# Splitting 49 output matmuls, moving the keys-values burst, and spreading the last stores in an attention-plus-MoE kernel

## Chip, cores, metric

One core of one Trainium2 chip. The metric is device time in microseconds (us). Before the change: 296.5 us (median of four runs, 296.09 to 296.61). All times are of fast runs unless said otherwise.

## The reference

```python
# attention: batch 8, heads 8, 576 positions, head size 64
r = np.maximum(x, 0.0); phi(x) = concat([r * cos_w, r * sin_w])      # for q and k
kv  = einsum('bhsf,bhsd->bhfd', phi(k), v);  z = sum(phi(k), axis=2)
x   = einsum('bhsf,bhfd->bhsd', phi(q), kv) / (einsum('bhsf,bhf->bhs', phi(q), z) + 1e-6)
# then, on 4608 tokens of 512:
h = x @ w_in                                # 512 -> 2048
g = h * (1 / (1 + exp(-beta * h)))
out = g @ w_out                             # 2048 -> 512, float32
```

## The kernel before

The 4608 tokens go in nine chunks of 512, numbered 0 to 8. For each chunk TensorE computes h in 16 *slots* (four matmuls of 512 columns each), ScalarE makes g of it, and TensorE forms the output. In chunks 0 and 1 the output is a plain product (`o_mm`); from chunk 2 on it is two fast products of seven sub-products each (`o_fast`, Strassen's scheme, 112 matmuls of 256 columns). In between stands the attention of the next batch: the keys-values burst `kv_all` (72 small matmuls), the numerators `num_all` (144), and the quotients `x_part` on VectorE. `raw_q` is the load of a later batch's q, and the `qt` transposes turn q by DMA. In `o_fast`, `m1` to `m7` are the seven products (x for the first pair of token tiles, y for the second), and `a3` to `a7` are VectorE's additions that combine their results, which TensorE leaves in banks of PSUM, its result memory. Of the code, `...` marks what is left out.

```python
def store(c, tt, o_sb, m0=0, m1=DM):
    for hf in range(2):
        bb, n = divmod((c * TCH + tt * P) // HP + hf, NQ)
        if c < 7 or (c == NTC - 1 and tt == 1):
            eng = nc.gpsimd
        else:
            eng = (nc.sync, nc.scalar)[hf] if (c, tt) == (NTC - 1, 3) else nc.sync
        eng.dma_start(out=out_v[bb, n][:, m0:m1], in_=o_sb[hf * HP : (hf + 1) * HP, m0:m1])

def o_mm(c, tt, jts):
    o_ps = ps[:, (2, 3, 0, 1)[tt] if c == 0 else 2 + tt % 2]
    for jt in jts:
        nc.tensor.matmul(o_ps, lhsT=gs[c, jt // 4][:, jt % 4, tt * P : (tt + 1) * P],
                         rhs=wout[:, jt, :], start=(jt == 0), stop=(jt == JT - 1))
    ...                                                   # copy and store when the last part is done

def att_q(b):
    q_relu(b, 0); q_relu(b, 1)
    q_turn_dma(b)                                         # transposes qb into qt, by DMA
    if b + 1 < B:
        load_raw(b + 1, "q")                              # 1152 KB

for slot in range(32):                                    # chunk 1
    if slot < 16:
        h_group(1, slot)
    else:
        o_part(1, (slot - 16) // 4, slot % 4)             # four o_mm steps
    one_unit(slot)

for c in range(2, NTC):
    b = c + 1
    for slot in range(16):
        h_group(c, slot)
        if slot == 0 and b < B:
            k_all(b); v_half(b, 1)
        if slot == 3 and b + 1 < B:
            att_q(b + 1)
        ...                                               # g_sums in slots 3, 7, 11, 13, 15
        if slot == 12 and b < B:
            kv_all(b)
    x, y = o_fast(c, 0, 6), o_fast(c, 1, 7)
    if b < B:
        for t, bank in enumerate((6, 0, 4)):
            num_all(b, t, bank)
        ...
        x_part(b, 0, 6)
    for n in (1, 5, 6, 2, 7, 3):
        x[f"m{n}"]()
        if n == 5 and b < B:
            x_part(b, 1, 0)
        if n == 6:
            x["a5"](); x["a6"]()
            if b < B:
                x_part(b, 2, 4)
    ...
```

## Time and profile before

| What | Before | How to read it |
|---|---|---|
| Time | 296.5 us | profiled run: span 294.5 us from first to last instruction |
| First numerator to next chunk's h, chunks 2 to 6 | 15.40, 15.94, 18.60, 14.27, 14.14 us | equal work, so every difference is waiting or a lower clock |
| TensorE gaps ahead of the fast products put down to "issue" | 6.7 us | "issue" means that the profile shows nothing that it waited for |
| TensorE clock | 0.5 from 165.18 to 168.59 us | the one slow slice of the run's middle |
| VectorE's last instruction to the common end | 6.3 us | 288.19 to 294.49 us |

The lines themselves stand in the prediction.

### The profile page before, as it was taken

The numbers are of one execution on the slowest core, as the hardware profiler recorded it, in microseconds if no ns is written. First come the engines' busy times: TensorE is split into PE (matmuls) and PEld (weight loads), VectorE is DVE, ScalarE is ACT, GpSimd is POOL, SyncE is SP. The second block draws the span as 40 slices with busy tenths as digits, with TensorE's granted clock in tenths as the row PEclk, the third lists the DMA queues.
The fourth block names the chain that finished last, engine by engine and source line by source line (L and its number), as shares of the span: only waits on it lengthen the run. The fifth ranks groups of instructions, "written<-read, shape, count | busy, mean of one in ns | idle before, by whom it ended". The sixth has DMA issues, their size and how long they took to land.

```text
span 294.5 us, 8004 instructions
## 1 busy us (share of the span) xinstructions
PE 276.2 (94%) x3369; PEld 174.8 (59%) x3376; DVE 197.4 (67%) x502; ACT 137.0 (47%) x228; POOL 75.7 (26%) x91
## 2 busy tenths in 40 slices
PE   8799999999999899989998699999999999999990
PEld 7454455455445585558645584578458845864780
DVE  5889975859996759675867469586858325424530
ACT  5678856861166314731384016621662177137510
POOL 1444000551760444035401424063400220000001
PEclk9999999999999999999999799999999999999997
DMA  7999999999999754984499246915301520050032
GB/s 250 376 392 373 394 344 358 293 269 322 245 252 302 218 121 97 321 235 96 88 361 237 56 98 177 297 31 126 73 2 29 125 73 0 20 124 1 2 72 71
DMA packets 50516, 53.94 MB, mean 183 GB/s; under 512 B 31200, under 2 KB 31472, under 8 KB 50480
## 3 DMA queue, kind: packets, MB, share of 16 engines
q1 hardware_dynamic: 47504, 45.69, 53.0%
q0 software_dynamic: 2784, 7.61, 9.9%
q8 instruction: 26, 0.43, 0.6%
q10 hardware_dynamic: 192, 0.14, 0.2%
q14 instruction: 10, 0.08, 0.1%
HBM read 36.71 MB, written 9.44 MB: 157 GB/s over the span
## 4 chain that ended last, share of the span: by engine, by line
PE 80%; DVE 9%; issue 5%; DMA 3%; SPq 1%; ACT 0%; POOL 0%; POOLq 0%; ACTq 0%; DVEq 0%
PE ps L374 41%; PE ps L440 28%; PE ps L420 5%; DMA raw_v<-in_v_dram 3%; PE ps L268 3%; PE ps L289 2%; DVE xs L311 2%; DVE vb L218 2%; DVE T L399 1%; SPq L79 1%; DVE rden L304 1%; DVE T L398 1%; DVE qb L193 0%; PE ps L348 0%; DVE win L115 0%
## 5 line engine op out<-in xcount | busy, mean ns | idle before, releaser
L374 PE MATMUL ps<-xt,win 128*128 128x512 bf16 (+1 forms) x580 | 127.3, 378 | 0.6 <-DVE vb L218 0.5
L382 ACT ACTIVATE g_t<-ps,beta 128x512 bf16<-128x512 f32 x144 | 98.6, 688 | 50.4 <-PE ps L374 48.3
L374 PEld LDWEIGHTS <-win 128*128 128x128 bf16 x580 | 56.0, 98 | 65.5 <-DMA xt<-xs 1.0
L415 POOL DMA_DIRECT2D out_dram<-o_sb x58 | 36.1, 629 | 127.6 <-issue 101.0
L440 PEld LDWEIGHTS <-S 128*128 128x128 bf16 x448 | 44.1, 99 | 11.4 <-issue 5.6
L221 POOL TENSOR_TENSOR qs<-qt,tanr 128x1152 bf16<-128x1152 bf16 x12 | 28.8, 2419 | 69.9 <-DVE den L300 55.6
L391 DVE TENSOR_TENSOR S<-g_t 128x512 bf16<-128x512 bf16 (+1 forms) x35 | 13.0, 371 | 37.5 <-ACT g_t L382 37.5
L440 PEld LDWEIGHTS <-g_t 128*128 128x128 bf16 x336 | 32.9, 99 | 6.8 <-issue 2.1
L440 PE MATMUL ps<-T,S 128*128 128x256 bf16 x224 | 28.1, 277 | 4.9 <-issue 4.9
L440 PE MATMUL ps<-wout,g_t 128*128 128x256 bf16 x224 | 30.1, 278 | 1.8 <-issue 1.8
L420 PE MATMUL ps<-wout,g_t 128*128 128x512 bf16 x121 | 28.3, 379 | 0.6 <-issue 0.3
L440 PE MATMUL ps<-wout,S 128*128 128x256 bf16 x224 | 27.0, 274 | 0.1
L470 ACT COPY o_sb<-ps 128x256 f32<-128x256 f32 x14 | 5.2, 372 | 46.3 <-PE ps L440 46.3
L311 DVE TENSOR_TENSOR xs<-ps,rden 128x768 bf16<-128x768 f32 (+4 forms) x26 | 22.8, 884 | 0.8
L218 DVE TENSOR_SCALAR vb<-raw_v,cos 128x256 bf16<-128x256 f32 x63 | 22.3, 402 | 0.0
L420 PEld LDWEIGHTS <-g_t 128*128 128x128 bf16 x128 | 12.1, 98 | 13.7
L460 ACT COPY p<-ps 128x256 f32<-128x256 f32 x14 | 5.2, 373 | 25.5 <-PE ps L440 25.5
L218 DVE TENSOR_SCALAR vb<-raw_v,sin 128x256 bf16<-128x256 f32 x54 | 14.7, 347 | 0.0
L440 PE MATMUL ps<-T,g_t 128*128 128x256 bf16 x112 | 14.5, 273 | 0.0
L394 DVE TENSOR_TENSOR S<-g_t,S 128x512 bf16<-128x512 bf16 (+1 forms) x35 | 13.0, 372 | 1.2
L497 DVE TENSOR_TENSOR o_sb<-ps,p 128x256 f32<-128x256 f32 x14 | 5.9, 425 | 11.3 <-PE ps L440 11.3
L289 PEld LDWEIGHTS <-qt 64*64 64x64 bf16 x576 | 10.4, 106 | 4.9 <-issue 3.7
(76 smaller groups left out, 238.5 us busy)
## 6 DMA issues: line engine op xcount, KB each, us to landing
raw_v<-in_v_dram SPq DMA_DIRECT2D x7, 1152.0 KB, 9.3
raw_k<-in_k_dram SPq DMA_DIRECT2D x7, 1152.0 KB, 7.6
raw_q<-in_q_dram SPq DMA_DIRECT2D x7, 1152.0 KB, 6.2
out_dram<-o_sb POOLq DMA_DIRECT2D x58, 128.0 KB, 2.7
w_stage<-in_moe_w_in_dram SPq DMA_DIRECT2D x3, 1024.0 KB, 14.0
w_stage<-in_moe_w_out_dram SPq DMA_DIRECT2D x2, 1024.0 KB, 7.6
w_stage<-in_moe_w_out_dram SPq DMA_DIRECT2D x4, 512.0 KB, 11.9
out_dram<-o_sb SPq DMA_DIRECT2D x12, 128.0 KB, 2.3
```

Source lines behind the costliest of these rows:

```text
L218: nc.vector.tensor_scalar(o, a, scalar1=t[:, n : n + 1], scalar2=None, op0=ALU.mult)
L221: return eng.tensor_tensor(dst.rearrange("q n (g p) -> q n g p", g=2), src.rearrange("q n (g p) -> q n g p", g=2), tanr[:, n0:n1].unsqueez ...
L268: nc.tensor.matmul(t[jj * HP : (jj + 1) * HP, g], lhsT=rk[hs, n, 2 * jp + jj, :], rhs=vb[hs, n, 2 * jp + jj].rearrange("q s e -> q (s e)") ...
L289: nc.tensor.matmul(ps[cols, bank + jj, slot * E : (slot + 1) * E], lhsT=(qts[b % 2], qs)[cs][rows, jp, n, cols], rhs=kv[rows, g, jp, cs, : ...
L311: nc.vector.tensor_tensor(o.rearrange("q j n s d -> q j (n s) d"), nv[:, :, a:z, :, 0:D].rearrange("q j n s d -> q j (n s) d"), rden[:, :, ...
L374: nc.tensor.matmul(ps[:, h_bank(c, jt), blocks.start * 64 : blocks.stop * 64], lhsT=win[jt // 4][:, mi, (jt % 4) * P : (jt % 4 + 1) * P], ...
L382: nc.scalar.activation(gs[c, jt // 4][:, jt % 4], ps[:, h_bank(c, jt)], AF.Silu, scale=beta[:, jt : jt + 1])
L391: nc.vector.tensor_tensor(s1, A21, A22, op=ALU.add)
L394: return nc.vector.tensor_tensor(s4, A12, s2, op=ALU.subtract)
L415: eng.dma_start(out=out_v[bb, n][:, m0:m1], in_=o_sb[hf * HP : (hf + 1) * HP, m0:m1])
L420: nc.tensor.matmul(o_ps, lhsT=gs[c, jt // 4][:, jt % 4, tt * P : (tt + 1) * P], rhs=wout[:, jt, :], start=(jt == 0), stop=(jt == JT - 1))
L440: nc.tensor.matmul(dst, lhsT=left(i), rhs=right[:, i], start=start and i == 0, stop=stop and i == JT // 2 - 1, skip_group_check=True)
```

## The change

Three edits. Forty-nine of chunk 1's output matmuls are cut into two column halves; `kv_all` goes from after h slot 12 to after h slot 10; the next-to-last tile of the last chunk is stored by SyncE and ScalarE in place of GpSimd. Neither of the first two removes work: the split adds 49 weight loads and 49 matmuls.

```diff
-            if c < 7 or (c == NTC - 1 and tt == 1):
-                eng = nc.gpsimd
-            else:
-                eng = (nc.sync, nc.scalar)[hf] if (c, tt) == (NTC - 1, 3) else nc.sync
+            eng = nc.gpsimd if c < 7 else (nc.sync, nc.scalar)[hf] if c == NTC - 1 and tt % 2 else nc.sync
-    def o_mm(c, tt, jts):
+    def o_mm(c, tt, jts, cols=1):
-            nc.tensor.matmul(o_ps, lhsT=..., rhs=wout[:, jt, :],
-                             start=(jt == 0), stop=(jt == JT - 1))
+            w = DM // cols if jt > 0 else DM
+            for m0 in range(0, DM, w):
+                nc.tensor.matmul(o_ps[:, m0 : m0 + w], lhsT=..., rhs=wout[:, jt, m0 : m0 + w],
+                                 start=(jt == 0), stop=(jt == JT - 1 and m0 == DM - w))
...                                                       # o_part hands cols on to o_mm
-            o_part(1, (slot - 16) // 4, slot % 4)
+            o_part(1, (slot - 16) // 4, slot % 4, 2 if slot > 18 else 1)
-            if slot == 12 and b < B:
+            if slot == 10 and b < B:
                 kv_all(b)
```

More of the change, by code (lines that the diff above doesn't have):

```diff
@@ L410, in store @@
             bb, n = divmod((c * TCH + tt * P) // HP + hf, NQ)
-            if c < 7 or (c == NTC - 1 and tt == 1):
-                eng = nc.gpsimd
-            else:
-                eng = (nc.sync, nc.scalar)[hf] if (c, tt) == (NTC - 1, 3) else nc.sync
+            eng = nc.gpsimd if c < 7 else (nc.sync, nc.scalar)[hf] if c == NTC - 1 and tt % 2 else nc.sync
             eng.dma_start(out=out_v[bb, n][:, m0:m1], in_=o_sb[hf * HP : (hf + 1) * HP, m0:m1])
-    def o_mm(c, tt, jts):
+    def o_mm(c, tt, jts, cols=1):
         o_ps = ps[:, (2, 3, 0, 1)[tt] if c == 0 else 2 + tt % 2]
         for jt in jts:
-            nc.tensor.matmul(o_ps, lhsT=gs[c, jt // 4][:, jt % 4, tt * P : (tt + 1) * P],
-                             rhs=wout[:, jt, :],
-                             start=(jt == 0), stop=(jt == JT - 1))
+            w = DM // cols if jt > 0 else DM
+            for m0 in range(0, DM, w):
+                nc.tensor.matmul(o_ps[:, m0 : m0 + w], lhsT=gs[c, jt // 4][:, jt % 4, tt * P : (tt + 1) * P],
+                                 rhs=wout[:, jt, m0 : m0 + w],
+                                 start=(jt == 0), stop=(jt == JT - 1 and m0 == DM - w))
         if jts[-1] < JT - 1:
@@ L427, in o_mm, with o_part @@
         store(c, tt, o_sb)
-    def o_part(c, tt, part):
-        o_mm(c, tt, range(4 * part, 4 * part + 4))
+    def o_part(c, tt, part, cols=1):
+        o_mm(c, tt, range(4 * part, 4 * part + 4), cols)
     def o_fast(c, pr, b_bank):
```

## The prediction

> **What bounds the kernel now.** I read the page's busy shares first, then who waited for whom, then the chain of waits piece by piece through chunks 2 to 4, then the windows by chunk, then the DMA queues and the end of the run.
>
> ```profile
> PE 276.2 (94%) x3369; PEld 174.8 (59%) x3376; DVE 197.4 (67%) x502; ACT 137.0 (47%) x228; POOL 75.7 (26%) x91
> PEclk9999999999999999999999799999999999999997
> q8 instruction: 26, 0.43, 0.6%
> ```
>
> TensorE is the bound: 94% busy, at full clock but for one slice in the middle. So the question is which TensorE gaps the change removes. Queue 8 matters later: 26 packets of 16 KB, 0.43 MB. From the waits:
>
> ```profile
> PE ps L440 <- issue: 6.7, 4, 3.0
> ```
>
> L440 holds the fast output products of chunks 2 to 8. TensorE stood still before them for 6.7 us in four pieces, and nothing visible released it: no semaphore, only "issue". The chain shows where three pieces lie (start, us, what):
>
> ```profile
> 97.40 1.36 PE ps L289 x137
> 98.76 3.06 PE ps L440 x26
> 101.82 1.35 issue
> 103.17 9.56 PE ps L440 x86
> ...
> 129.16 2.08 PE ps L440 x17
> 131.24 1.90 issue
> 133.14 10.53 PE ps L440 x95
> ...
> 160.10 1.09 PE ps L440 x9
> 161.19 2.99 issue
> 164.18 13.09 PE ps L440 x103
> ```
>
> The reader should look at the matmul counts before each gap: 26, 17, 9. A fourth gap of 0.45 us follows in chunk 5 after the first row of L440. Each matmul has a weight load, so these are about 52, 35, 18 and 1 instructions into L440: 17 fewer per chunk. The built program says why. One chunk has 785 TensorE instructions (h 128, keys-values 144, numerators 288, fast products 224, one semaphore), and 785 = 3 x 256 + 17. Numbering all TensorE instructions, the four gaps fall at places 194 to 195 modulo 256. So the gaps are the edges of 256-instruction blocks[...]. TensorE waits for its **own instructions**. The trace's records of queue 8 agree: packets start at 100.75, 130.66, 161.91 and 191.69, work resumes at 103.17, 133.14, 164.18 and 194.14, thus 2.3 to 2.5 us after the packet's start (about 1.0 us of it the packet itself).
>
> The windows give what this costs per chunk, from the first numerator to the next chunk's h (window, PE, PEld, DVE, ACT, POOL busy, PEclk, DMA share, GB/s):
>
> ```profile
> 97.33:112.73 15.40, 14.05 (x258) 12.29 (x258) 10.64 (x31) 2.18 (x5) 6.85 (x6) 1.00 0.55 145
> 127.73:143.67 15.94, 14.04 (x258) 12.37 (x258) 10.72 (x31) 2.18 (x5) 6.86 (x6) 1.00 0.52 143
> 158.66:177.26 18.60, 15.61 (x258) 13.17 (x258) 10.83 (x31) 2.18 (x5) 6.85 (x6) 0.91 0.44 117
> 192.25:206.52 14.27, 13.82 (x258) 12.46 (x258) 10.58 (x31) 2.17 (x5) 6.86 (x6) 1.00 0.37 81
> 221.51:235.65 14.14, 14.05 (x258) 12.39 (x258) 8.46 (x23) 2.18 (x5) 2.07 (x4) 1.00 0.37 81
> ```
>
> Same work each time. Chunk 6 has no instruction gap and takes 14.14 us. Its one gap, about 0.3 us before the seventh product, waits for VectorE's a6. Chunk 4 pays twice: 2.99 us of gap, then 3.41 us at half clock (the clock record is 0.5 from 165.18 to 168.59).
>
> [...]the trace behaves as if one block is fetched ahead.
> [...]in chunks 2 to 4 its packet starts only as the 1152 KB load of raw_q runs dry (100.7, 130.6, 161.7)[...].
> [...]Only the longest gap, 2.99 us, is followed by a half-clock stretch, of 3413 ns.
> [...]Here 64 L420 matmuls take 13.83 us (216 ns each) and 16 L440 matmuls of 256 columns 1.74 us (109 ns).
>
> **The change, part by part.**
> *Split.* 49 L420 matmuls of chunk 1 become 98 with 98 weight loads: 98 more TensorE instructions before chunk 2. Direct cost: 49 x (2 x 109 - 216) = 49 x 2 ns = 0.1 us; a weight load of 98 ns fits beside a 109 ns matmul. Its real effect is that each later block edge falls 98 instructions earlier in the work.
> *Keys-values burst.* It goes from after h slot 12 to after slot 10; its inputs are long ready (in chunk 3 VectorE ends the sine scaling at 117.1, slot 10 ends near 122). No work is added. Before the numerators 40 h instructions instead of 24 now stand, 20 matmuls x 216 ns = 4.32 us instead of 2.6 us, so an edge crossed near the burst leaves more time.
> I counted the new places in the built program. In chunks 2, 3, 4, 5, 6 the edge is numerator instruction 242, 225, 208, 191, 174 of 288; the edge before it is 14, 31, 48, 65, 82 instructions ahead of the numerators. The sequencer runs some 50 instructions ahead of TensorE (my estimate, from late fetches with quiet DMA), so the fetch starts about 64 instructions ahead in chunk 2, in the tail of the burst: 4.5 us before the numerators. The edge is reached 242/288 x 1.36 = 1.1 us into them. That leaves 5.7 us, where before chunk 2 had (98.76 + 3.06 - 97.4) = 4.4 us. Needed: 2.4 us plus the start of the packet, so it must start within about 3.3 us. What it meets is not raw_q, which comes about 2 to 4 us later, but the qt transposes (92.5 to 96.7 in chunk 2). A packet that waits for all of them starts near 97, would be usable at 99.4, and is needed at 98.5: up to 0.9 us lost in chunk 2, less in 3 and 4, nothing in 5 and 6; the first 0.4 us of each costs nothing, since the VectorE wait of chunk 6 absorbs it. I take 0.3 us in all.
> Gain against the 14.14 us chunk: 1.26 + 1.80 + 4.46 + 0.13 = 7.65 us. Chunk 4's 4.46 is the gap and the half clock together.
> *Stores.* The next-to-last store (chunk 8, tile 1) leaves GpSimd for SyncE and ScalarE. In the chain's end:
>
> ```profile
> 287.86 0.52 POOL out_dram L415
> 288.38 0.51 POOLq L814
> ```
>
> The trace shows GpSimd's closing drain from 288.28 to 293.71, while SyncE has seen all its own stores land by 291.66 and waits. The common end follows 0.75 us later, at 294.5. With GpSimd's last store in chunk 7, its drain should be over long before, and SyncE sets the end: 291.66 + 0.75 = 292.4. The new issues (0.47 to 0.55 us each, near 287.35) are done before the last halves are due at 288.2. Gain: 2.05 us.
> Sum: -7.65 - 2.05 + 0.3 + 0.1 = -9.3 us. 296.56 - 9.3 = **287.3 us**.
>
> **The rivals.**
> A: *the wait only moves.* The fetch, caught behind the transposes and then raw_q, arrives late inside the numerators. For it: in chunk 2 a fetch behind raw_v started its packet only at 92.66[...]. Against it: the earlier burst buys 1.7 us, and edges later in the sequence of chunks are ever safer. It would give back 1 to 2 us in each of chunks 2 to 4: 290 to 293 us, more if a half-clock stretch comes with it.
> B: *VectorE takes over.* Without gaps the a6 wait of chunk 6 may appear in every chunk. I have included it by taking 14.14 us; if VectorE falls back further, 0.3 us a chunk: 288.5 us.
> C: *no instruction fetch at all, only DMA or VectorE timing*, and the split is a plain cost. Then only the stores gain: about 294.6 us. The modulo-256 match of four gaps speaks strongly against it.
> D: *the end doesn't move*, because the stores land later on the two hardware queues: 289.3 us.
>
> **Range and chances.** All gaps gone, with a slightly better end: 286. One or two chunks keep a gap of 1 us, or the end fails: 290. So 285.9 to 290.2. Over 2% faster means below 290.6: 0.84. Within 2% needs rival A in force or C: 0.14. Slower needs new gaps longer than the old: 0.02.
>
> **What would show it.** Right: "issue" before L440 drops from 6.7 us to under 1; no half-clock slice before the end; chunks 2 to 6 alike at 14.0 to 14.5 us; queue 8 packets in each chunk starting before the numerators; the chain ending in SyncE or ScalarE, with 4 to 5 us between the last matmul and the end instead of 7. Wrong: gaps inside the numerators (L289) at places 194 modulo 256, raw_q again ahead of the fetch, or the last drain still about 5 us.

The trace of the kernel before shows this of blocks and fetches. Queue 8, of kind "instruction", moved 26 packets of 16384 bytes while 6745 matmuls and weight loads were recorded, one packet for 259. From the packet of chunk 2's gap to that of chunk 3's, 768 instructions on (785 less 17), there are three: 100.75, 104.80 and 121.45, then 130.66. Counting back 256 instructions from each gap gives the edge before it: in chunks 2 to 4 the packet starts 3.06, 2.66 and 3.04 us after TensorE reaches that edge. In chunk 6, where the packet at 219.63 is all that the DMA queues move from 214 to 222 us, it starts 1.95 us before TensorE is there, some 33 instructions ahead. The trace doesn't show when a fetch is asked for; the 50 instructions of the prediction are an estimate: these 33, and what TensorE gets through in the unknown time from the asking to the packet's start.

## The result, and the profile after

The changed kernel takes 285.36 us (median of four, 284.85 to 285.78), against 296.5 us before: ratio 0.9626, 95% interval 0.9607 to 0.9645. A ratio here is the mean time of one kernel's fast runs over that of the other's of the same rounds, so not quite the ratio of the medians. The prediction said 287.3 us with a range of 285.9 to 290.2. Its direction and mechanism held; the gain was larger than its range allowed.

The page of the changed kernel, busy shares and TensorE clock:

```profile
PE 275.7 (97%) x3425; PEld 178.9 (63%) x3425; DVE 197.8 (70%) x502; ACT 137.0 (48%) x228; POOL 74.7 (26%) x89
PEclk9999999999999999999999999999999999999999
```

TensorE does the same 276 us of work in a shorter span, and no slice is below 90% of the clock. From the table of waits, after:

```profile
PEld L439 <- issue: 1.3, 5, 0.3
PE ps L374 <- DMA xt<-xs: 0.8, 1, 0.8
```

L439 is the line that was L440. Its matmuls no longer wait for "issue" at all; what is left of it is five small waits of weight loads. The windows from the first numerator to the next h, chunks 2 to 6, columns as in the prediction:

```profile
97.20:111.33 14.13, 14.04 (x258) 12.39 (x258) 10.55 (x31) 2.18 (x5) 6.86 (x6) 1.00 0.54 145
126.32:140.45 14.13, 14.04 (x258) 12.38 (x258) 10.54 (x31) 2.18 (x5) 6.86 (x6) 1.00 0.48 131
155.44:169.57 14.13, 14.04 (x258) 12.37 (x258) 10.55 (x31) 2.18 (x5) 6.86 (x6) 1.00 0.50 126
184.56:198.69 14.13, 14.04 (x258) 12.37 (x258) 10.55 (x31) 2.18 (x5) 6.85 (x6) 1.00 0.42 82
213.69:227.81 14.12, 14.04 (x258) 12.37 (x258) 8.44 (x23) 2.18 (x5) 2.07 (x4) 1.00 0.45 81
```

All five are alike. The sum went from 78.35 to 70.64 us, a gain of 7.71 us.

The chain of waits in chunk 3, after (start, us, what):

```profile
126.43 0.70 ACT g_t L382
...
130.76 0.41 DVE p L481
131.17 0.34 DVE u L484
131.55 8.89 PE ps L439 x80
```

Where "issue" pieces stood, the chain now runs over ScalarE's last g, VectorE's sums, quotients, a5 and a6 into the seventh product: the short wait that only chunk 6 showed before. The end of the chain, after:

```profile
275.96 3.94 PE ps L439 x36
279.91 0.02 issue
279.93 0.42 DVE o_sb L496
```

VectorE's last instruction ends at 280.36 us and the span at 283.75: 3.39 us instead of 6.30, a gain of 2.91 us. The other parts of the span hardly move: the start of chunk 2's h goes from 82.18 to 82.05 us, the last two chunks take 52.55 instead of 52.54 us. So 7.71 + 2.91 + 0.1 = 10.7 us, which is the difference of the two spans (294.49 to 283.75).

### The profile page after: what moved, and what is told of

Same layout as the page of the kernel before. It is cut to its first block, busy times and chain, and to the rows that moved or that the text cites.

```text
span 283.7 us, 8110 instructions
## 1 busy us (share of the span) xinstructions
PE 275.7 (97%) x3425; PEld 178.9 (63%) x3425; DVE 197.8 (70%) x502; ACT 137.0 (48%) x228; POOL 74.7 (26%) x89
## 4 chain that ended last, share of the span: by engine, by line
PE 76%; DVE 12%; DMA 6%; issue 3%; ACT 1%; SPq 1%; DVEq 0%
PE ps L374 43%; PE ps L439 24%; PE ps L419 5%; DVE xs L311 3%; DMA raw_v<-in_v_dram 3%; PE ps L268 3%; DMA xt<-xs 2%; DVE rden L304 1%; ACT g_t L382 1%; DVE T L399 1%; SPq L79 1%; DVE p L481 1%; PE ps L289 1%; DVE T L398 1%; DVE den L300 1%
## 5 line engine op out<-in xcount | busy, mean ns | idle before, releaser
L412 POOL DMA_DIRECT2D out_dram<-o_sb x56 | 35.1, 632 | 69.8 <-issue 43.2
L439 PEld LDWEIGHTS <-S 128*128 128x128 bf16 x448 | 43.8, 98 | 7.0 <-issue 1.3
L439 PEld LDWEIGHTS <-g_t 128*128 128x128 bf16 x336 | 32.5, 98 | 4.3
L419 PE MATMUL ps<-wout,g_t 128*128 128x256 bf16 (+1 forms) x177 | 29.3, 320 | 0.0
L439 PE MATMUL ps<-wout,g_t 128*128 128x256 bf16 x224 | 29.1, 273 | 0.0
L439 PE MATMUL ps<-T,S 128*128 128x256 bf16 x224 | 27.3, 272 | 0.0
L439 PE MATMUL ps<-wout,S 128*128 128x256 bf16 x224 | 26.7, 272 | 0.4
L419 PEld LDWEIGHTS <-g_t 128*128 128x128 bf16 x177 | 16.9, 98 | 9.2
L439 PE MATMUL ps<-T,g_t 128*128 128x256 bf16 x112 | 14.5, 273 | 0.0
L289 PEld LDWEIGHTS <-qt 64*64 64x64 bf16 x576 | 10.4, 106 | 4.9 <-issue 3.7
```

The lines of the kernel that those rows point to most:

```text
L289: nc.tensor.matmul(ps[cols, bank + jj, slot * E : (slot + 1) * E], lhsT=(qts[b % 2], qs)[cs][rows, jp, n, cols], rhs=kv[rows, g, jp, cs, : ...
L419: nc.tensor.matmul(o_ps[:, m0 : m0 + w], lhsT=gs[c, jt // 4][:, jt % 4, tt * P : (tt + 1) * P], rhs=wout[:, jt, m0 : m0 + w], start=(jt == ...
L439: nc.tensor.matmul(dst, lhsT=left(i), rhs=right[:, i], start=start and i == 0, stop=stop and i == JT // 2 - 1, skip_group_check=True)
```

## The experiments

The theory under test: TensorE's instructions are fetched in blocks of 256 (one packet for 259 recorded), about one block ahead; a fetch waits in the DMA queues behind the data that is there (2.66 to 3.06 us in chunks 2 to 4 of before); the numerators (288 instructions in 1.36 us) use up a block faster than a late fetch brings the next (2.3 to 2.5 us from a packet's start to use); and the split matters only by moving the block edges 98 instructions. The "edge" is the place where the next block is first needed, and it is "crossed" when TensorE gets there. The trace records when a fetch packet starts, not when it was asked for: that moment is inferred throughout. Rivals are named with each run. Each call of runs had its own chip and its own runs of the kernel before; medians below are of fast runs.

| Run | Time, us | Before on that chip, us | Ratio (95%) |
|---|---|---|---|
| stores alone (e1) | 293.2 | 295.86 | 0.9895 (0.984 to 0.995) |
| split and burst (e2) | 288.8 | 295.86 | 0.9758 (0.971 to 0.981) |
| split alone (e3) | 289.2 | 295.86 | 0.9786 (0.973 to 0.984) |
| burst alone (e4) | 296.2 | 295.86 | 1.0024 (0.996 to 1.009) |
| 15 split, not 49 (e5) | 296.8 | 295.34 | 1.0019 (0.992 to 1.011) |
| raw_q later, no split (e6) | 289.7 | 295.34 | 0.9789 (0.970 to 0.987) |
| split in h instead (e7) | 288.8 | 295.34 | 0.9771 (0.969 to 0.986) |
| 16 columns on GpSimd (e9) | 288.2 | 295.34 | 0.9733 (0.966 to 0.981) |
| changed kernel again (e11) | 285.7 | 295.70 | 0.9654 (0.963 to 0.968) |
| a6 first (e8) | 285.1 | 295.70 | 0.9648 (0.962 to 0.968) |
| no split, all else (e10) | 286.7 | 295.70 | 0.9710 (0.967 to 0.975) |

### The stores alone (e1, and e12 for a profile)

```diff
# the kernel before, with the new store() only
```

> The kernel before with only the store queues changed (last chunk, tile 1, from GpSimd to SyncE and ScalarE). Theory: the end after VectorE's last instruction shrinks from 6.3 us to the 3.4 us that the changed kernel shows, nothing else moves: about 293.5 us, the three 'issue' gaps of 1.35, 1.90 and 2.99 us and the half-clock stretch stay. Rival (the sum of the prediction): only GpSimd's drain goes, 2.05 us: 294.5 us.

Measured: the fast runs took 293.64, 291.69 and 293.16 us. The fourth run, the profiled one, fell in a slow state (321.93 us, clock 0.85), so I ran the kernel once more for a profile:

> The stores alone once more, because the profile of the first such run fell in the slow state. Theory: the gaps of about 1.4, 1.9 and 3.0 us at the same places as before the change, the common end 3.4 us after VectorE's last instruction instead of 6.3, 293.5 us.

Measured: one run, 292.85 us (its state is unknown, being a single run; mean clock 0.992). Its profile has TensorE's "issue" gaps (6.5 us in four pieces) and a half-clock stretch of 3.41 us from 163.50, both as before the change. The common end comes 3.41 us after VectorE's last instruction. So the stores alone shorten the end by 2.9 us, not by the 2.05 us of my sum.

### The split and the burst without the stores (e2)

```diff
# the changed kernel, with the old store()
```

> The changed kernel with the old store queues. Theory: all instruction gaps gone as in the changed kernel (chunks 2 to 6 at 14.13 us from the first numerator to the next h), the old end of 6.3 us after VectorE's last instruction: 285.4 + 3.0 = about 288.4 us. If the gains of the two halves did not add, it would differ from that by over 0.5 us.

Measured: 288.84 us. Chunks 2 to 6 follow each other at 29.11 to 29.12 us as in the changed kernel, and the end is the old one, 6.29 us. The two halves add up: the instruction gaps and the end are independent.

### The split alone (e3)

```diff
# the changed kernel, with the old store() and
-            if slot == 10 and b < B:
+            if slot == 12 and b < B:
```

> The split alone: keys-values burst back in slot 12, old stores. The block edges sit at numerator instruction 242, 225, 208, 191, 174 as with the burst moved; the fetch is asked for some 1.5 us later than with the burst in slot 10. Theory (the fetch waits behind the qt transposes anyway, so asking earlier gains nothing): at most 0.7 us of gap in chunk 2, little elsewhere, 288.4 to 289.2 us. Rival (the earlier burst is what makes the fetch arrive in time): gaps of 1 to 2.5 us in the numerators of chunks 2 to 4, 290 to 295 us.

Measured: fast runs of 288.77, 289.24 and 290.74 us (one slow run left out). The chain shows what is left without the earlier burst:

```profile
125.91 1.09 PE ps L289 x106
127.00 0.35 issue
...
155.21 1.03 PE ps L289 x96
156.23 0.71 issue
```

Both gaps lie inside the numerators (L289), at places 195 and 194 modulo 256 of TensorE's instructions. The theory put up to 0.7 us in chunk 2; it came in chunks 3 and 4 instead (0.35 and 0.71 us). The size was right, the place was not. The rival, that the burst is what makes the fetch arrive in time, is wrong as to nearly all of the gain: the burst's move is worth 0.7 us of the profiles (from the first h of chunk 2 to VectorE's last instruction 198.99 us here, 198.28 us in e2), and in time e3 and e2 cannot be told apart.

### The burst alone (e4)

```diff
# the kernel before, with
-            if slot == 12 and b < B:
+            if slot == 10 and b < B:
```

> The burst in slot 10 alone, no split, old stores. Theory: the block edges stay at instruction 52, 35, 18 and 1 of the fast products, the edge before them still inside the numerators, so the fetch is asked for at the same moment and meets the same raw_q load: the gaps of 1.35, 1.90, 2.99 and 0.45 us stay and the time is 296.5 us within 0.6. Rival (the burst's move relieves VectorE or the DMA queues by itself): over 2 us faster.

Measured: 296.2 us, ratio 1.0024, unchanged. Its chain has the old gaps after the old counts (26, 17):

```profile
99.28 3.06 PE ps L440 x26
102.34 1.28 issue
...
129.61 2.08 PE ps L440 x17
131.68 2.15 issue
```

So the move does nothing where the edges lie badly. The half-clock stretch this time begins at 133.89, right after chunk 3's gap, and none follows chunk 4's longer one (2.54 us).

### Fifteen split matmuls instead of forty-nine (e5)

```diff
# e3, with
-            o_part(1, (slot - 16) // 4, slot % 4, 2 if slot > 18 else 1)
+            o_part(1, (slot - 16) // 4, slot % 4, 2 if 18 < slot < 23 else 1)
```

> Only 15 instead of 49 output matmuls split, burst in slot 12, old stores: 30 more TensorE instructions instead of 98. Theory (block edges count, not the split): the edge of chunk 2 now falls 22 instructions, 11 matmuls, into the fast products, with the edge before it at numerator 54, so its fetch meets raw_q: a gap of about 3.2 us there, after 11 matmuls at a place 194 modulo 256, perhaps followed by 3.4 us of half clock; chunk 3 (edge 5 instructions into the fast products, fetch asked for before raw_q) at most 0.4 us, chunks 4 to 6 under 0.4. About 292 to 294 us. Rival (splitting matmuls helps by itself, so fifteen of them bring a good part): no gap of over 1 us in chunk 2, 289 to 291 us.

Measured: 296.8 us (one slow run left out), no gain at all. The chain of this kernel:

```profile
99.04 1.31 PE ps L442 x11
100.35 3.28 issue
...
131.25 0.33 PE ps L442 x2
131.58 2.37 issue
```

In chunk 2 the gap stands where the count put it, after 11 matmuls, and is as long as expected (3.28 against 3.2 us). This decides against any benefit of the split as such: fifteen split matmuls bring nothing where forty-nine, alone as well, bring 6 to 7 us (e3). My numbers for chunks 3 and 4 were wrong: I expected at most 0.4 us each and got 2.37 and 2.87. In the trace, chunk 3's transposes end and raw_q starts near 128.3, with the edge before the gap crossed at 129.95. By my estimate the fetch was asked for at about 128.4. Its packet starts only at 131.70, as raw_q runs dry. So, if the estimate holds, it just missed the free moment. The estimate of "50 instructions ahead" is too coarse to place an event within half a microsecond, and by the same estimate the miss cost 3.3 us here, from 128.4 to 131.70.

### Raw_q out of the way, no split (e6)

```diff
# the kernel before; att_q(b + 1, load=False) in the chunk loop, and after the third quotient part:
                 if b < B:
                     x_part(b, 2, 4)
+                if b + 2 < B:
+                    load_raw(b + 2, "q")
```

> The kernel before with one thing changed: the load of raw_q for the next batch is issued after the third quotient part of the chunk, not before the numerators (no split, burst in slot 12, old stores). The edges stay at 52, 35, 18, 1. Theory (the fetch is late because it queues behind raw_q): the packet starts about 1 us after it is asked for, the gaps of 1.35 and 1.90 us vanish, that of 2.99 us falls to under 1 us, no half-clock stretch; 289 to 290.5 us. Rival (the fetch itself is slow, whatever the data queues hold): the gaps stay, 296 us.

Measured: 289.7 us with every instruction where it was before, save the one load. The chain in chunks 3 and 4:

```profile
128.12 2.08 PE ps L440 x17
130.20 0.04 issue
130.24 10.58 PE ps L440 x95
...
157.24 1.09 PE ps L440 x9
158.33 0.80 issue
```

Compare the prediction's lines: after the same 17 and 9 matmuls the gaps fell from 1.90 to 0.04 us and from 2.99 to 0.80 us. Chunk 2 has no such gap either. The fetch packets now start 1.1, 0.9 and 0.8 us after the crossing of the edge (at 99.01, 127.86 and 156.78), not 2.7 to 3.1 us. No half-clock stretch comes before the end. The packets themselves take 0.93 to 0.96 us, against 0.97 to 0.99 before, so it is the start that moved. This shows the cause directly: with nothing but raw_q's load moved, the packets start 1.8 to 2.2 us sooner after the edge. Of the "issue" waits before the fast products 1.1 us are left (chunks 4 and 5).

### The same count, split elsewhere (e7)

```diff
# e2, but cols=2 only for the very last output matmul of chunk 1, and in h_mm:
+            for bl in ((slice(0, 4), slice(4, NB)) if c == 1 and mi > 0 else (blocks,)):
```

> The changed kernel with old stores and the split at another place: 48 of chunk 1's h matmuls and one output matmul split into halves, the same 98 added instructions before chunk 2. Theory: as the 49 split output matmuls with old stores, 288.8 us within 0.6, chunks 2 to 6 again 29.12 us each. Rival (the output matmuls of chunk 1 gain by being split): gaps return or the time differs by more than 1 us.

Measured: 288.78 us, as e2. The chunks follow at 29.11 to 29.13 us. (The profiled run was the longest of four, 291.51 us; it had reached chunk 2 2.8 us later than e2's profiled run, with a half-clock stretch of 3.41 us in the start-up, at 17 us.) So between these two places it does not matter which matmuls are split, only how many instructions they add ahead of chunk 2.

### Sixteen columns left on GpSimd (e9)

```diff
# the changed kernel; columns m1-16 to m1 of the first half of (last chunk, tile 1) by nc.gpsimd,
# the rest by the engine that the changed kernel names
```

> The changed kernel, but 16 of 512 columns of half of the next-to-last tile again stored by GpSimd. Theory: GpSimd's closing drain is long after any late store of its own, so the common end comes about 6.3 us after VectorE's last instruction as before (about 288.2 us), while SyncE has seen all stores land about 2.6 to 2.9 us after it, not 3.5 us as before, because the big software-queue packets are gone. Rival (the drain's length follows the bytes of the store): the end comes within 4.5 us, under 286.5 us.

Measured: 288.17 us, as the theory's time, but partly by luck: the profiled run took 287.37 us, and its end came 5.44 us after VectorE's last instruction: neither the 6.3 us of the theory nor under 4.5. The trace explains the difference. GpSimd's closing drain took 5.27 us here and 5.43 us before, so its length hardly depends on the bytes (4 KB here, 256 KB before), but with one store to issue late instead of two it began 0.60 us *before* VectorE's last instruction ended, not 0.09 us after. In the changed kernel the same drain takes 5.34 us, from 229.32 to 234.66, and harms nobody. The other half of the theory held: SyncE had seen every store land 2.75 us after VectorE's last instruction, against 3.47 before and 2.63 in the changed kernel.

### VectorE's a6 first (e8), beside the changed kernel (e11)

```diff
# the changed kernel, with
-            if n == 5 and b < B:
-                x_part(b, 1, 0)
             if n == 6:
                 x["a5"](); x["a6"]()
                 if b < B:
+                    x_part(b, 1, 0)
                     x_part(b, 2, 4)
```

> The changed kernel unaltered, as the yardstick for the two that follow on the same chip: 285.4 us within 0.7, ratio to before about 0.963.

> The changed kernel with VectorE's order altered: the two additions after the third product (a5, a6) ahead of the second quotient part. TensorE's order, and with it every block edge, is as in the changed kernel. Theory (the 0.25 us that TensorE still waits before the seventh product in chunks 2 to 6 is VectorE being late with a6): five such waits go, 14.13 us per chunk become 13.9, 1.2 us faster than the changed kernel: about 284.2 us. Rival (VectorE then is late elsewhere, or the wait is PSUM's and not a6's): same as the changed kernel within 0.4 us.

Measured: the changed kernel 285.71 us, a6 first 285.14 us, intervals that overlap: no difference shown. The wait before the seventh product is gone as expected, but the chunks shorten only from 29.12 to 29.05 us. In chunk 3 a pause of about 0.18 us now stands after the first product of the second pair, ahead of the product that reuses the PSUM bank that a7 reads; a7 comes behind both quotient parts now. I did not test that link by itself. The rival "VectorE then is late elsewhere" fits best.

### No split, everything else (e10)

```diff
# the kernel before, with raw_q later (e6), the burst in slot 10, the new store(), a6 first (e8)
```

> No split, but raw_q issued later, the burst in slot 10, the new stores and a6 first. Theory: the edges stay at 52, 35, 18 and 1 of the fast products; with raw_q out of the way only 0.8 us (chunk 4) and 0.2 us (chunk 5) of instruction gap are left, so it lands about 1 us above the kernel with the split and a6 first: 285.2 us. If it is over 287 us, another wait has come with moving raw_q.

Measured: 286.7 us, 1.5 us above e8 (expected 1; the two intervals just touch). Gaps remain at the old edges of chunks 3 and 4; "issue" ahead of the fast products is 1.2 us in all. So nearly the same time is to be had without the split, and no version that I ran clearly beats the changed kernel.

## Why the prediction was right and wrong

**Right: the cause of the gaps.** Block edges at 194 modulo 256 and a fetch behind the data: e5 moves the gap to the counted place, e6 removes it by moving one load, e7 gets the same from other split matmuls. The first rival, a wait that only moves, showed in small in e3 and in full in e5. The third, no instruction fetch at all, falls with e5 and e7, and the fourth, an end that doesn't move, with e12.

**Right: the gain of the chunks.** I said 7.65 us less 0.3 us of leftover gap; it was 7.71 with none left. The leftover was not needed, but narrowly, and in part by luck: in chunk 2 the fetch packet started at 95.66 us. With the 2.3 to 2.5 us that the prediction measured from a packet's start to use, the block was usable about 98.0 to 98.2 us, and TensorE reached it at 98.21. The packets of chunks 2 to 4 (95.66, 124.12, 153.21) started as the qt transposes ran out, so this part of the step was as predicted; only the transposes ended near 95.9 us, not 96.7. By the same sum a packet 0.8 us later would have come 0.5 to 0.7 us too late.

**Right: VectorE's a6.** Chunks 2 to 6 each take 14.12 to 14.13 us, as chunk 6 did before (14.14); the wait is in each of them.

**Wrong: the size of the end.** The step that failed is "SyncE sets the end: 291.66 + 0.75 = 292.4 ... Gain: 2.05 us". It measured 2.91 us. The mechanism was right, GpSimd's drain was last and went away, but I carried SyncE's own finish over unchanged, 3.47 us after VectorE's last instruction. It became 2.63 us. Kernels that keep GpSimd's 256 KB store have 3.44 to 3.75 us (e2 to e7), those with none 2.57 to 2.65 us, and 4 KB left on GpSimd give 2.75 us (e9). So GpSimd's large store in flight, not its drain, held back the last half-tiles by about 0.8 us. In the trace of before, the last store's packets on ScalarE's queue start only from about 290.0 us, 1.8 us after their issue at 288.22, and GpSimd's 4096-byte packets run from 288.95 to 290.7; after, the first of them start about 1.4 us after theirs. That they wait for one another's packets is read from these times; e9 shows only that the wait goes when all but 4 KB leave GpSimd's queue. I had seen those transfers in the profile and not asked what else they held back.

**Wrong: the split and the margin.** The 0.1 us of the split did not show: TensorE waits 0.8 us for the transposed xt at the start of chunk 2 anyway, where before it waited 0.5 us (put down to VectorE's vb). Terms in all: 0.86 (end), 0.36 (chunks), 0.1 (split) and 0.1 (start) make the 1.4 us by which the profiled span beat my sum of 9.3. The rest, up to the 1.9 us between 287.3 and 285.4, is the spread of runs: the profiled run of the changed kernel was the slowest of its four. My lower bound assumed only "a slightly better end"; it should have let the end fall by as much as its widest term was unsure. One sign was off for the same reason: the last matmul is 3.85 us from the end, not 4 to 5.

**Which gaps the half clock followed.** My trials compare the gaps' whole lengths, which don't decide it: it came after 2.99 us (before) and 2.15 us (e4), and not after 2.54 (e4), 3.28 and 2.87 us (e5). The clock records, read again, order all of these. In the profile of before the changes of the clock lie whole multiples of 3.413 us apart: 46 such windows at full clock, 1 at half, 36 at full; the changed kernel has 81 at full. Cut the traces into such windows: TensorE stood still for 2.41 us of the window that ends where the half clock begins in before, 2.15 us in e4, 2.65 us in e12. The gap of 3.28 us in e5 lies across a border and leaves 1.75 and 1.53 us, the one of 2.87 us 1.04 and 1.83, the one of 2.54 us in e4 1.06 and 1.48; the gap of 1.90 us (before) lies in one window. None of these was followed by the half clock. So the idle time within one window tells these gaps apart: 2.15 us and more was followed by the half clock, 1.90 us and less was not. This order was worked out after the runs and tested by none, and the start-up of e7 does not fit: there 1.36 us of idle time was enough, which stays open.

## What to carry to other kernels

Where a TensorE that is the bound stands still for "issue", number its instructions and take the places modulo 256: a constant, as the 194 to 195 here, suggests that it waits for its own program. What helped here was to move a large load out of the way, or to shift the edges by some instructions. A shift must be counted for every chunk that follows, since 30 instructions gained nothing where 98 gained 6 to 7 us, and any later edit of TensorE's stream moves the edges again. At the end of a kernel, ask of a last transfer both what waits for it and what it holds back. GpSimd's closing drain took 5.43 us after a late store of 256 KB (before), 5.27 us after one of 4 KB (e9) and 5.34 us with none (the changed kernel); in the first two it set the end.
